# A list of tokens with rows of 64 bytes instead of 4, filled during the scan

## The chip, the core and the metric

The kernel runs on one core of a Trainium2 chip. The core has five engines with queues of their own: TensorE (PE in the profile), VectorE (DVE), ScalarE (ACT), GpSimd (POOL) and SyncE (SP). SP computes nothing here; it issues the plain DMA transfers and loads registers. POOL issues the indirect ones, gathers and scatters whose rows are chosen by indices, beside arithmetic of its own. All transfers run on the same 16 DMA engines. The metric is the device time of one execution, in microseconds. The kernel before took 819.09 us, the median of three runs (815.78 to 823.08).

## The reference

A scan over time with a matrix as state, for 4 x 8 heads, 768 steps and 40 dimensions, and behind it a layer of 8 experts of which each token uses one. In short:

```python
for t in range(S):                                 # S=768, state is D x D for each (batch, head)
    y[:, :, t] = einsum('bhd,bhde->bhe', r[t], state)
    Sa = einsum('bhde,bhe->bhd', state, a[t])
    state = state * w[t][:, :, None, :] - outer(Sa, b[t]) + outer(v[t], k[t])
x = y.transpose(0, 2, 1, 3).reshape(3072, 320)
logits = x @ w_gate + modality_bias[modality_id]   # 8 experts
e_idx = argmax(logits, axis=1)
gate_w = softmax(logits)[arange(N), e_idx]
for e in range(8):
    mask = e_idx == e
    out[mask] = gate_w[mask, None] * (maximum(x[mask] @ w1[e], 0) @ w2[e])   # 320 -> 1024 -> 320
```

## The kernel before

**The scan.** The 768 steps are cut into 24 chunks of 32; two chunks make a pair, for which the inputs are loaded together. Within a chunk the recurrence is solved as a triangular system: a Gram matrix of the inputs is formed on PE (`gram`), masked, written to a scratch tensor in DRAM (`scr`), and read back in another layout (`L<-scr`) for a group of one or two pairs. There it is inverted by elimination (`eliml`, 31 steps of a product and a subtraction: `tmpP`, `L`). The first two groups are eliminated on DVE, the others on POOL (the last one half on each). The result goes out to DRAM (`scrT<-L`), comes back in the layout PE needs (`TT<-scrT`, 32 KB each), and is multiplied into the chunk (`ps_tr<-rs,TT`). There is one buffer for `L`, so the read of the next group waits for the write of this one. Each chunk passes a state `Z` on to the next.

**The gate.** When a pair of chunks is done its outputs `xo` (256 tokens, as two halves of 128 partitions) go through `gate(m,x)`, for m from 0 to 11: logits on PE, the maximum, a one-hot of the expert, and, by products with a triangular matrix and with a running count, the rank of each token within its expert. Expert times 3,072 plus rank is the token's place in the list `lst` in DRAM, `pi`. Two indirect scatters on POOL, one for each half, write the 128 token numbers (`ids`, a constant) to those places. The outputs themselves go to the DRAM tensor `xs`, with the gate's weight in front.

**The list.** `lst` has 29,440 entries of one int32: 8 stretches of 3,072 and a reserve. At the start of the kernel all of it is filled with a number out of range (`BIG`), by one transfer from a tile of 128 x 230; a gather skips such rows. So an expert's tokens can be taken in slots of 256 entries, and places that nobody wrote do no harm. A scatter to `lst` waits until the scatter ahead of it has landed, since both write the same tensor.

**The experts.** A slot takes 256 entries of the list (`idx<-lst`, an SP transfer with a start known only at run time), gathers those rows of `xs` (POOL), splits inputs and weights into two parts for products in fp32r (ACT copies the high part, DVE or POOL subtracts it, L1129 among these), multiplies, and scatters the rows to the output (POOL, L1157). Slots -2 and -1 are prepared within the scan (`early`, after gate m=8, from the 2,304 tokens known by then); their weights lie in tiles that the scan no longer needs. Twelve slots follow. In slot -2 two of the subtractions are given to POOL (`oc=(1,3)`).

**What sets the order.** The scan and the gates are not written in the order they run. A planner (`Sched`) records each instruction with its inputs and outputs, gives each a cost and an urgency (the longest chain of work that hangs on it), and goes forward in modelled time: each engine takes, among the instructions that could start first, the most urgent. SP's transfers share a modelled DMA bandwidth, and a transfer may be put no more than 2 us ahead of it. The order that comes out is fixed for each engine in the program. A transfer that needs nothing and is due late, such as the zeroing of the rows of `xs` that the early slots could touch (`blank`, `xs<-wrm`), is therefore issued when SP has nothing more urgent. Instructions emitted by the planner all have line L381 in the profile. The work of `__init__` comes before the planner's, and the experts' (lines from L1089) are written out by hand.

Of the kernel before, what the change touches and what calls it, by code (L numbers as in the profile page):

```python
# [438 lines left out]
H,S=8,768; XW=324  # L439
# [15 lines left out]
def phase_a(S,ctx,rt,rm,bk,v,w,a,emit_x,pp,ident,kp):  # L455
    nc=S; tc=S.tc; NX=OPT['NX']
# [132 lines left out]
    def xtr(m,q,kd):  # L589
        def one(p):  # L590
            if p==0:
                st['trX']=pst(f"trX{m}_{q}_{kd}",[128,4,4,32])
                if kd==0: st['XT',m,q]=spt("XT",[128,4,4,2,32],f"XT{m}_{q}",OPT['nXT'])
            tr=st['trX']
            nc.tensor.transpose(tr[:,p],st['b',m][:,kd,512*q+128*p:512*q+128*p+128],ident)
            if p==3: nc.scalar.copy(st['XT',m,q][:,:,:,kd,:],tr)
        return [lambda p=p: one(p) for p in range(4)]
# [197 lines left out]
    def go(l):  # L795
        for f in l: f()
# [8 lines left out]
    with contextlib.nullcontext():  # L805
        loadw(0); loada(0); loadb(0); loadw(1)
        go(prep_wl(0,0)); amul(0,0); prep_bk(0,(0,),'b')
        w01=prep_wl(0,1); go(w01[:2]); prep_bk(0,(0,),'k'); go(w01[2:]); amul(0,1); prep_bk(0,(1,))
        loada(1); loadb(1); loadw(2)
        def dums(k_):  # L810
            pass
        go(prep_ab(0,0)); go(xtr(0,0,0)); dums('b'); go(xtr(0,0,1)); dums('c'); g00=gram(0,0); g01=gram(0,1)
        go(prep_ab(0,1)); go(xtr(0,1,0)); go(g00[:7]); go(xtr(0,1,1)); dums('d'); go(prep_wl(1,0)); go(g00[7:]); go(g01[:7]); w11=prep_wl(1,1); go(w11[:3]); go(g01[7:]); go(w11[3:])
        amul(1,0); prep_bk(1,(0,),'b','V'); prep_bk(1,(0,),'k'); amul(1,1); prep_bk(1,(1,))
        e0=eliml(0); e0[0](); loada(2); loadb(2); stack(0); stack(1)
        go(prep_wl(2,0)); go(prep_wl(2,1)); loadw(3); loadr(0); vload(0); vload(1)
        k0=31 if 0 in OPT['HB'] else 6
        go(e0[1:k0])
        go(prep_ab(1,0)); go(xtr(1,0,0)); go(xtr(1,0,1)); dums('e'); go(gram(1,0))
        go(prep_ab(1,1)); go(xtr(1,1,0)); go(xtr(1,1,1)); dums('f'); go(gram(1,1)); dums('g')  # L820
        amul(2,0); prep_bk(2,(0,)); amul(2,1); prep_bk(2,(1,))
        go(prep_ab(2,0)); go(xtr(2,0,0)); go(xtr(2,0,1)); dums('h'); go(gram(2,0)); dums('i')
        go(prep_ab(2,1)); go(xtr(2,1,0)); go(xtr(2,1,1)); go(gram(2,1))
        late2(); loada(3); e1=eliml(1); e1[0](); loadb(3)
        go(e1[1:OPT['EJ']+1])
        go(e0[k0:31]); e0[31](); go(ftr(0)); go(ftr(1)); go(ftr(2)); ttload(0); ttload(1); go(lv(0))
        for q in range(2): go(prep_wl(3,q))
        loadw(4); amul(3,0); amul(3,1); prep_bk(3); loada(4)
        go(prep_ab(3,0)); xg(3,0); go(ftr(3))
        go(e1[OPT['EJ']+1:])  # L830
# [58 lines left out]
PSUM=bass.MemoryType.PSUM; DRAM=bass.MemoryType.DRAM  # L889
NT,D,E,F=3072,320,8,1024  # L890
NTL=NT//128; SL=256; NSL=NT//SL+E-1; NS0=14
LIST=E*NT+NSL*SL; BIG=1<<20
XW=324
MOPT=dict(eb=100,wb=0,em=8,ns0=NS0,gxb=1,MS=('PE','Activation','DVE','Pool'),oc=(0,1,2,3),ow=(),lag=2,pf=0,hb=3,ob=4,
 tb=5,pf0=4, own=[[('q',1),('c',0)],[('c',1)],[('q',2)],[('c',2)],[('q',3)],[('c',3)],[],[]],
# [4 lines left out]
class Moe:  # L900
    def __init__(self,tc,ctx,modality_id,w_gate,mbias,w1,w2,out,ptr,ident):
# [3 lines left out]
        self.gp=ctx.enter_context(tc.tile_pool(name="mgt",bufs=1))  # L905
        dp=ctx.enter_context(tc.tile_pool(name="mdp",bufs=1,space=DRAM))
        self.xs=dp.tile([NT,XW],F32,name="xs")
        self.lst=dp.tile([LIST,1],I32,name="lst")
        self.slt=None

        self.cum=[cp.tile([128,2,E],BF16,name=f"cum{i}") for i in range(2)]
        tctx=ExitStack(); tp=tctx.enter_context(tc.tile_pool(name="mtmp",bufs=1))
        fill=tp.tile([128,LIST//128],I32,tag="fill",name="fill"); nc.gpsimd.memset(fill,BIG)
        nc.sync.dma_start(self.lst.rearrange("(p f) o -> p (f o)",p=128),fill)
        self.wg=cp.tile([128,3,32],F32,name="wg"); nc.gpsimd.memset(self.wg,0.0)
        nc.sync.dma_start(self.wg[:,0:2,0:E],w_gate[0:256].rearrange("(c p) e -> p c e",p=128))
        nc.sync.dma_start(self.wg[64:128,2,0:E],w_gate[256:320])
# [32 lines left out]
        tctx.close()  # L950
        nc.vector.memset(self.cum[0][:,0],0.0); self.S=None
        self.nw=0; self.em=MOPT['em']
    def blank(self,z):

        k=NTL//2-1-self.em
        v=self.xs.rearrange("(c q n) e -> c q (n e)",c=2,q=2)[:,:,64*(self.em+1)*XW:]
        for c in range(2):
            for q in range(2): self.S.sync.dma_start(v[c,q].rearrange("(p a b) -> p a b",p=128,b=81),z[:,0:81].unsqueeze(1).broadcast_to([128,2*k,81]))

    def gate(self,m,x):  # L960
# [34 lines left out]
        pi=t("pi",[128,2],I32)  # L995
        ps=t("ps",[128,2]); nc.vector.tensor_reduce(ps,pv,axis=AX.X,op=ALU.add)
        nc.vector.tensor_copy(pi,ps)
        if m==NTL//2-1: S.boost=1e6
        if m<NTL//2-1: S.slk=SOPT['sll']
        for i in range(2):  # L1000
            nc.gpsimd.indirect_dma_start(self.lst,Off(pi[:,i:i+1].bitcast(U32)),self.ids[:,12*i+m:12*i+m+1],None)
        S.boost=0.0; S.slk=SOPT['slg']
        sm=t("sm",[128,2]); nc.vector.tensor_reduce(sm,ex,axis=AX.X,op=ALU.add)
        nc.vector.tensor_scalar(sm,sm,1e-9,None,op0=ALU.add)
# [48 lines left out]
    def early1(self,R,i,n):  # L1053
# [14 lines left out]
            S.call('sync','load',f,[f"reg{i}_{k}"],[ti])  # L1068
        load(0,LIST-SL); load(1,E-1)
        idx=t("ix",[128,2],I32,2)  # L1070
        S.call('sync','dma_dyn',lambda c,rs: c.sync.dma_start(rs(idx),self.lst[bass.ds(val[i,0],SL)].rearrange("(b p) o -> p (b o)",p=128)),[idx],[f"reg{i}_0",self.lst])
        xg=[S.inst(R[1],f"xg_e{i}{b}",[128,XW],o) for b,o in enumerate([[0,324],[648,972]][i])]
        for b in range(2): nc.gpsimd.indirect_dma_start(xg[b],None,self.xs,Off(idx[:,b:b+1].bitcast(U32)),bounds_check=NT-1,oob_is_err=False)
        self.first.append((idx,xg))
# [2 lines left out]
    def _run(self,ctx,wpool,pool,ph,po):  # L1077
# [12 lines left out]
        def prep(s):  # L1090
            base=nc.values_load(self.tab[0:1,s:s+1],engines=(SP,),min_val=0,max_val=LIST-SL,skip_runtime_bounds_check_because="computed from counts that sum to the number of tokens")
            ex=nc.values_load(self.tab[0:1,NSL+s:NSL+s+1],engines=(SP,),min_val=0,max_val=E-1,skip_runtime_bounds_check_because="clamped to the last expert")
            idx=idxs[s%4]
            nc.sync.dma_start(idx,self.lst[bass.ds(base,SL)].rearrange("(b p) o -> p (b o)",p=128))
            x=xg[s%4]
            if s<4:
                for b in range(2): nc.gpsimd.memset(x[b],0.0)
# [213 lines left out]
```

## Time and profile before

| | |
|---|---|
| median of 3 runs | 819.09 us |
| profiled execution, time | 814.86 us |
| its span, first to last instruction | 812.9 us |
| mean granted TensorE clock | 0.826 |
| busy: PE, DVE, ACT, POOL | 598.3, 504.5, 388.1, 273.5 us |
| list scatters | 24, first 184.92 us, last 578.63 us |
| `idx<-lst` | 12 in the experts, 2 early |
| DMA engines, mean share by queue | SP's 53.1%, POOL's 3.0% |

Times within the profile are microseconds from the start of the span. A row of the timeline has start, length, engine, line, operation, the tile written and the tiles read, the count, and in brackets the idle time of the engine before it and what ended that. A row of the waits has the engine, the line and what it wanted, what it waited for, then the total, the number of times and the longest. In the list of DMA issues the last number of POOL's rows is the median time from the issue to the landing. "issue" as a releaser means that the profile shows nothing that the engine waited for.

### The profile page before, as it was taken

How to read it: one execution, taken by the hardware profiler on the slowest of the kernel's cores; microseconds unless marked ns; L12 is line 12 of the kernel's file. 1: busy time of each engine (PE TensorE's matmuls, PEld its weight loads, DVE VectorE, ACT ScalarE, POOL GpSimd, SP SyncE). 2: the span in 40 equal slices, each digit the busy share in tenths (PEclk: the TensorE clock that was granted, in tenths of full speed). 3: DMA queues.
4: the chain of work that ended last, by engine and by line, in shares of the span. 5: the costliest groups of instructions: out<-in, count | busy, mean ns of one | idle time of the engine just before them, and what ended most of it. 6: DMA issues, size and time to landing. Idle time of an engine off the chain costs nothing. (4 is left out here: it accounts for less than half of the span.)

```text
span 812.9 us, 25308 instructions
## 1 busy us (share of the span) xinstructions
PE 598.3 (74%) x10527; PEld 535.1 (66%) x10527; DVE 504.5 (62%) x1260; ACT 388.1 (48%) x814; POOL 273.5 (34%) x435
## 2 busy tenths in 40 slices
PE   0652789946577677778824677885679999999992
PEld 0542677835566566666614556764679999999992
DVE  5694845863248846675621563656768888888850
ACT  1662154731457355554521524543546666666640
POOL 8440038314181582055625300200234222322210
PEclk9966586876879899797955757986889999999997
DMA  2979231555726529663479557736099755776500
GB/s 57 334 221 165 64 74 47 176 156 46 46 68 179 166 62 149 132 104 54 62 55 60 51 35 123 196 45 143 18 303 283 224 174 184 238 234 213 178 33 14
DMA packets 103480, 104.97 MB, mean 129 GB/s; under 512 B 65806, under 2 KB 86464, under 8 KB 101824
## 3 DMA queue, kind: packets, MB, share of 16 engines
q1 hardware_dynamic: 99904, 95.35, 53.1%
q0 software_dynamic: 3456, 7.93, 3.0%
q8 instruction: 85, 1.39, 1.1%
q14 instruction: 35, 0.29, 0.1%
HBM read 88.46 MB, written 15.99 MB: 128 GB/s over the span
## 5 line engine op out<-in xcount | busy, mean ns | idle before, releaser
L381 POOL TENSOR_TENSOR tmpP<-L 128x30 f32<-128x30 f32 (+9 forms) x135 | 70.8, 525 | 165.2 <-DMA L<-scr 155.5
L381 ACT COPY XZ<-BK 32x640 f32<-32x640 f32 x96 | 69.4, 723 | 31.9 <-PE ps_tr L381 22.1
L381 POOL TENSOR_TENSOR L<-L,tmpP 128x30 f32<-128x30 f32 (+9 forms) x135 | 73.4, 544 | 9.9
L381 POOL DMA_INDIRECT lst<-ids,pi x24 | 24.5, 1023 | 153.9 <-DMA lst<-ids,pi 69.5
L1150 PE MATMUL os<-l,hh 128*128 128x320 f32 x208 | 65.7, 316 | 11.5 <-POOL l L1129 11.3
L381 PE MATMUL ps_tr<-rs,TT 64*64 64x40 f32 x896 | 42.0, 256 | 42.6 <-DMA TT<-scrT 35.1
L1142 ACT ACTIVATE hh<-h 128x256 fp32r<-128x256 f32 x104 | 40.0, 384 | 68.9 <-PE h L1138 68.7
L381 DVE COPY U<-ps_tr 32x320 f32<-32x320 f32 x56 | 27.6, 492 | 70.2 <-PE ps_tr L381 53.8
L381 PEld LDWEIGHTS ps_tr<-rs,TT 64*64 64x64 f32 x896 | 37.8, 166 | 49.3 <-DMA TT<-scrT 25.2
L1138 PE MATMUL h<-xh,h 128*128 128x256 f32 x224 | 66.9, 299 | 2.2 <-ACT h L1120 1.4
L1151 PE MATMUL os<-h,hl 128*128 128x320 f32 x208 | 65.1, 313 | 0.0
L1138 PE MATMUL h<-xh,l 128*128 128x256 f32 x224 | 64.9, 290 | 0.3 <-DVE l L1121 0.3
L1149 PE MATMUL os<-h,hh 128*128 128x320 f32 x208 | 64.9, 312 | 0.0
L1138 PE MATMUL h<-xl,h 128*128 128x256 f32 x224 | 64.5, 288 | 0.0
L381 ACT COPY U<-ps_tr 32x320 f32<-32x320 f32 x56 | 23.3, 415 | 83.9 <-DVE U L381 54.3
L381 DVE TENSOR_TENSOR xo<-ps_tr,H 32x320 f32<-32x320 f32 x96 | 46.7, 487 | 24.9 <-PE ps_tr L381 14.6
L1143 DVE SCALAR_TENSOR_TENSOR hl<-h,hh 128x256 fp32r<-128x256 f32 x104 | 44.0, 423 | 24.4 <-ACT hh L1142 23.2
L1157 POOL DMA_INDIRECT out_dram<-o,idx x24 | 26.9, 1123 | 90.8 <-DVE hl L1143 29.2
L381 PE MATMUL ps_tr<-ident,BK 128*128 128x128 f32 x192 | 38.8, 354 | 15.7 <-DVE BK L381 11.9
L381 ACT COPY XZ<-ps_tr 40x320 f32<-40x320 f32 x92 | 38.6, 420 | 20.8 <-PE ps_tr L381 19.4
L381 PE MATMUL tz<-U,XZ 64*40 64x40 f32 x1472 | 32.4, 234 | 21.5 <-ACT U L381 8.5
L1150 PEld LDWEIGHTS os<-l,hh 128*128 128x128 f32 x208 | 40.0, 192 | 12.2 <-POOL l L1129 11.8
(204 smaller groups left out, 1687.4 us busy)
## 6 DMA issues: line engine op xcount, KB each, us to landing
r<-in_moe_w_dram SPq DMA_DIRECT2D x13, 1280.0 KB
r<-in_moe_w_dram SPq DMA_DIRECT2D x13, 1024.0 KB
BK<-in_bk_dram SPq DMA_DIRECT2D x12, 1024.0 KB
r<-in_moe_w_dram SPq DMA_DIRECT2D x26, 256.0 KB
A<-in_a_dram SPq DMA_DIRECT2D x12, 512.0 KB
U<-in_v_dram SPq DMA_DIRECT2D x48, 128.0 KB
ws<-in_w_dram SPq DMA_DIRECT2D x24, 165.5 KB
xs<-xo SPq DMA_DIRECT2D x24, 162.0 KB
```

Of the source, the lines that this page charges most:

```text
L381: else: r=getattr(getattr(nc,eng),name)(*[rs(x) for x in a],**{n:rs(x) for n,x in k.items()})
L1138: for i,(a,b) in enumerate(k): nc.tensor.matmul(hp,a,b,start=(i==0),stop=(i==len(k)-1))
L1142: nc.scalar.activation(hh,hp,AF.Relu)
L1143: nc.vector.scalar_tensor_tensor(hl,hp,0.0,hh.bitcast(F32),op0=ALU.max,op1=ALU.subtract)
L1149: nc.tensor.matmul(os[b],hh[:,sl],h2[:,f],start=(f==0),stop=False)
L1150: nc.tensor.matmul(os[b],hh[:,sl],l2[:,f],start=False,stop=False)
L1151: nc.tensor.matmul(os[b],hl[:,sl],h2[:,f],start=False,stop=(f==7))
L1157: nc.gpsimd.indirect_dma_start(self.out,bass.IndirectOffsetOnAxis(ap=idx[:,b:b+1].bitcast(U32),axis=0),o,None,bounds_check=NT-1,oob_is_err ...
```

## The change

A row of `lst` gets 16 int32 columns, 64 bytes, of which only the first is read. The gate copies the token numbers of its two halves to a tile of 128 x 2 x 16 on DVE (`idw`), each number 16 times, and a scatter writes rows of 16. The reads of the list take column 0, so they still move 256 elements of 4 bytes, now 64 bytes apart.

The list is 16 times as large, 1.88 MB. It is no longer filled in `__init__` but by a method `fill`, recorded with the planner among the loads of the third pair of chunks: one SP transfer that writes a tile of 128 x 115 (460 bytes a partition, set once) 32 times over to each partition's share. The tile is kept instead of being given back after `__init__`. What is computed is the same.

```diff
-        go(prep_ab(2,1)); go(xtr(2,1,0)); go(xtr(2,1,1)); go(gram(2,1))
+        emit_x.fill(); go(prep_ab(2,1)); go(xtr(2,1,0)); go(xtr(2,1,1)); go(gram(2,1))
...
-LIST=E*NT+NSL*SL; BIG=1<<20
+LW=16; LIST=E*NT+NSL*SL; BIG=1<<20
...
-        self.lst=dp.tile([LIST,1],I32,name="lst")
+        self.lst=dp.tile([LIST,LW],I32,name="lst")
...
-        fill=tp.tile([128,LIST//128],I32,tag="fill",name="fill"); nc.gpsimd.memset(fill,BIG)
-        nc.sync.dma_start(self.lst.rearrange("(p f) o -> p (f o)",p=128),fill)
+        self.fw=LIST//256; self.fil=cp.tile([128,self.fw],I32,name="fill"); nc.gpsimd.memset(self.fil,BIG)
...
+    def fill(self):
+
+        self.S.sync.dma_start(self.lst.rearrange("n o -> (n o)").rearrange("(p r f) -> p r f",p=128,r=2*LW),self.fil.unsqueeze(1).broadcast_to([128,2*LW,self.fw]))
...
+        idw=t("idw",[128,2,LW],I32); nc.vector.tensor_copy(idw,self.ids[:,m:m+13:12].unsqueeze(2).broadcast_to([128,2,LW]))
...
-            nc.gpsimd.indirect_dma_start(self.lst,Off(pi[:,i:i+1].bitcast(U32)),self.ids[:,12*i+m:12*i+m+1],None)
+            nc.gpsimd.indirect_dma_start(self.lst,Off(pi[:,i:i+1].bitcast(U32)),idw[:,i],None)
...
-        S.call('sync','dma_dyn',lambda c,rs: c.sync.dma_start(rs(idx),self.lst[bass.ds(val[i,0],SL)].rearrange("(b p) o -> p (b o)",p=128)),[idx],[f"reg{i}_0",self.lst])
+        S.call('sync','dma_dyn',lambda c,rs: c.sync.dma_start(rs(idx),self.lst[bass.ds(val[i,0],SL),0:1].rearrange("(b p) o -> p (b o)",p=128)),[idx],[f"reg{i}_0",self.lst])
...
-            nc.sync.dma_start(idx,self.lst[bass.ds(base,SL)].rearrange("(b p) o -> p (b o)",p=128))
+            nc.sync.dma_start(idx,self.lst[bass.ds(base,SL),0:1].rearrange("(b p) o -> p (b o)",p=128))
```

## The prediction

> **What bounds the kernel now.** I read the page first, for where the tensor engine (PE) is full and where it is not.
>
> ```profile
> span 812.9 us, 25308 instructions
> PE   0652789946577677778824677885679999999992
> ```
>
> A slice is 20.3 us. From slice 30 (about 595 us) PE is full to the end: the expert stage is bound by PE there, and nothing in the change touches it. The open time lies before, in the scan. So the next view was the waits in total, and then the DMA issues with their time to landing.
>
> ```profile
> POOL lst L381 <- DMA lst<-ids,pi: 69.5, 9, 10.4
> POOL lst L381 <- issue: 40.4, 8, 12.0
> PE os L1150 <- POOL l L1129: 11.3, 2, 6.2
> ...
> lst<-ids,pi POOLq DMA_INDIRECT x24, 10.0
> out_dram<-o,idx POOLq DMA_INDIRECT x24, 3.7
> ```
>
> GpSimd (POOL) stands 109.9 us in front of list scatters, in 17 waits, because a scatter may not start before the one ahead has landed (the profile names no releaser for the second row, but its waits have the same length). A list scatter takes 10.0 us to land though it writes 128 times 4 bytes; the scatter of output rows, also 128 writes but of 1,280 bytes each, takes 3.7. More bytes land sooner, so the 10 us belongs to the 4-byte write and not to the issue on POOL or the count of rows.
>
> Whether that costs time is read from the stages. I laid the timeline of POOL beside windows of all engines:
>
> ```profile
> 184.92 1.17 POOL L381 DMA_INDIRECT lst<-ids,pi  x1 [0.17 <-DVE U L381]
> 197.71 1.01 POOL L381 DMA_INDIRECT lst<-ids,pi  x1 [9.81 <-issue]
> 209.88 1.00 POOL L381 DMA_INDIRECT lst<-ids,pi  x1 [6.80 <-DMA lst<-ids,pi]
> ...
> 398.24 1.00 POOL L381 DMA_INDIRECT lst<-ids,pi  x1 [0.23 <-DVE pv L381]
> 408.80 1.00 POOL L381 DMA_INDIRECT lst<-ids,pi  x1 [8.11 <-DMA lst<-ids,pi]
> 421.04 1.00 POOL L381 DMA_INDIRECT lst<-ids,pi  x1 [8.54 <-DMA lst<-ids,pi]
> ...
> 476.95 1.00 POOL L381 DMA_INDIRECT lst<-ids,pi  x1 [11.79 <-DVE e_n L381]
> ```
>
> The windows' columns are length, then busy us of PE, its weight loads, DVE, ACT and POOL, the clock, the DMA share and GB/s:
>
> ```profile
> 192.00:197.50 5.50, 0.00 (x0) 0.00 (x0) 0.00 (x0) 0.00 (x0) 0.00 (x0) 0.80 0.26 22
> 218.50:222.50 4.00, 0.00 (x0) 0.00 (x0) 0.00 (x0) 0.00 (x0) 0.00 (x0) 1.00 0.83 38
> 404.50:408.50 4.00, 0.00 (x0) 0.00 (x0) 0.00 (x0) 0.00 (x0) 0.00 (x0) 0.80 0.62 33
> 418.50:434.50 16.00, 0.00 (x0) 0.00 (x0) 0.00 (x0) 0.00 (x0) 1.00 (x1) 0.50 0.78 55
> 486.00:489.00 3.00, 0.00 (x0) 0.00 (x0) 0.00 (x0) 0.00 (x0) 0.00 (x0) 0.97 0.65 33
> ...
> 184.92:590.00 405.08, 281.07 (x6628) 236.83 (x6629) 219.97 (x600) 180.53 (x381) 139.73 (x235) 0.78 0.57 90
> 100.00:184.92 84.92, 67.89 (x1655) 57.27 (x1655) 52.90 (x128) 43.41 (x92) 36.31 (x73) 0.76 0.40 112
> ```
>
> Five times every engine stops. Each stop lies inside the 11 us after a scatter (from 184.92, 209.88, 398.24, 408.80 with 421.04, and 476.95), and next to no bytes move meanwhile (22 to 55 GB/s). So a scatter in flight holds up not only POOL but the other transfers, and with them whatever waits for those. The last two rows give the same as a rate: PE is busy 0.80 of the scan before the first scatter, and 0.69 from there to 590.
>
> **Part 1: the scatter lands sooner.** Nothing in this trace writes 64-byte rows to memory. Below, the nearest are writes in runs of 128 bytes (a block of 32 floats), two issues of 512 runs each:
>
> ```profile
> 107.56 0.86 SPq L381 DMA_DIRECT2D scr<-G  x2
> ...
> 109.94 0.34 SPq L381 DMA_DIRECT2D L<-scr  x1
> ```
>
> The read L<-scr needs what these write, so 1,024 runs of 128 bytes landed within 2.4 us of the first issue. From above it is the 10.0 us of today. I take 3.8, next to the 3.7 of the output scatter, which is of the same kind and count; so each of 24 landings loses 6.2 us, with 2.4 and 10.0 as the ends. POOL's own instruction stays near 1.0 us.
>
> The Trainium skill speaks against this. Its page "DMA: Bandwidth & Descriptors", section Specifications, has 512 bytes as the least transfer for full rate, with a read-modify-write below it. By that rule 64 bytes is no better than 4, and the landing stays at 10.0. The 128-byte rows above bear it out badly. It is a rival below.
>
> Each stop can lose what its scatters lose, at most its own length: 5.5 + 4.0 + 4.0 + 3.0 for the four that are shorter than 6.2, and 2 x 6.2 = 12.4 of the 16.0, which has two scatters in it. Its chain is this:
>
> ```profile
> 412.53 0.35 SPq L381 DMA_DIRECT2D scrT<-L  x1
> ...
> 421.96 0.32 SPq L381 DMA_DIRECT2D TT<-scrT  x1
> ...
> 434.98 1.28 PE L381 MATMUL ps_tr<-rs,TT 64*64 64x40 f32 x14 [17.07 <-DMA TT<-scrT]
> ```
>
> The eliminated block is written out, read back and used, each a transfer, and a scatter runs beside the first and another beside the second. Further down the same two legs are quoted without a scatter (97.81 to 100.89 for the write): 3.1 us instead of 9.4, with half the bytes. The five stops give 28.9 us. What could come late next is the block itself: it is computed on POOL, and it too is held by the scatters, so it moves earlier with them. I take the 28.9 whole and leave out the smaller gaps (PE alone idle), to pay for what surfaces behind. Ends: 10 us, if the recurrence of the scan takes up two thirds; and the whole loss of rate, 405.08 - 281.07 / 0.80 = 53.5 us, which has part 2's first stall in it.
>
> **Part 2: the passage to the experts.** The last gate's two scatters stand in POOL's queue in front of two subtractions (L1129) of the first expert's weights:
>
> ```profile
> 568.70 1.33 POOL L381 DMA_INDIRECT lst<-ids,pi  x1 [11.79 <-DVE w L1125]
> 578.63 1.06 POOL L381 DMA_INDIRECT lst<-ids,pi  x1 [8.60 <-DMA lst<-ids,pi]
> ...
> 591.25 1.26 POOL L1099 DMA_INDIRECT xg<-xs,idx  x1 [9.23 <-issue]
> ...
> 588.25 0.38 SPq L1094 DMA_DIRECT2D idx<-lst  x1
> ...
> 581.46 0.64 PE L1150 MATMUL os<-l,hh 128*128 128x320 f32 x1 [6.22 <-POOL l L1129]
> ...
> 595.45 0.63 PE L1150 MATMUL os<-l,hh 128*128 128x320 f32 x1 [5.07 <-POOL l L1129]
> ```
>
> With 3.8 the second scatter goes at 572.5, the first subtraction ends at 575.6 instead of 581.4, and PE's 6.2 us goes. The list's read follows its last landing: 576 instead of 588.25, the gather 579 instead of 591.25, and the second subtraction is done 12 us earlier against a PE that comes 6.2 earlier, so the 5.1 goes too. Together 11.3 us. Next late would be DVE's copies of the same weights; PE is full from 595 on.
>
> **Part 3: the fill.** It writes 1.88 MB in 4,096 runs of 460 bytes instead of 118 KB once at the start. It needs nothing from the scan and is due at the first scatter (184.92). The planner treats the zeroing of the token rows (xs<-wrm) alike, which is due later still, and issues it when SP first has nothing more pressing, so I expect the fill just there, ahead of it:
>
> ```profile
> xs<-wrm SPq DMA_DIRECT2D x4, 243.0 KB
> ...
> 65.03 1.29 SPq L381 DMA_DIRECT2D xs<-wrm  x2
> ...
> 67.30 1.14 SPq L381 DMA_DIRECT2D scrT<-L  x1
> ...
> 76.64 5.88 SPq L381 DMA_DIRECT2D TT<-scrT  x8
> ...
> 97.81 0.51 SPq L381 DMA_DIRECT2D scrT<-L  x1
> ...
> 100.89 4.15 SPq L381 DMA_DIRECT2D TT<-scrT  x8
> ```
>
> This is a bad place: scrT to TT takes 9.3 us beside the zeroing and 3.1 without, and all of PE waits. 972 KB in 3,072 runs cost 6.3 us; the fill costs 6.3 x 4096/3072 = 8.3 by runs, 6.3 x 1.94 = 12.1 by bytes. If it pushes the zeroing behind the reads, 6.3 comes back. Ends 0 (a slot where nothing hurries) and 12.1; I take the middle, 6. Queued behind it on SP's rings: A, scrT, and the TT reads.
>
> **Part 4: the copies and the reads.** Twelve copies of 128x32 on DVE:
>
> ```profile
> 417.83 0.17 DVE L381 COPY xo<-sm 128x8 f32<-128x8 f32 x1
> ```
>
> At 0.2 us each that is 2.4 us, of a DVE busy 220 of 405 us; the copies read only constants and can go in any gap. The scatter waits for them, but they stand long before it. I take 1, ends 0 and 2.4. The list's reads stay 256 elements of 4 bytes, now 64 apart: 3.0 us today (588.25 to 591.25), taken as unchanged, a microsecond either way.
>
> **Sum.** -28.9 - 11.3 + 6 + 1 = -33.2. The profiled execution took 814.86 us (span 812.9), so 781.7; the median of the three runs, 819.09, is 4.2 above that execution, so 786 in its terms, and all times below are in its terms.
>
> **Rivals.**
> - *The scan gives more.* All of the lost rate comes back: 53.5 + 5.1 - 7 = 51.6, so 767. For it: POOL's 109.9 us of waits, much of it inside the elimination that PE then waits for. Against: the recurrence, which also holds the scan before the first scatter at 0.80.
> - *Only the passage gains.* The stops come back behind something else in the same order of work: -11.3 + 7, so 815, no measurable change. For it: the order on every engine is planned anew with a 1.88 MB transfer and twelve copies in it. Against: in the stops nothing is running that could be the next bound.
> - *The 64-byte write is no faster, and the fill is paid.* Place: the TT reads at 76.64, behind the fill; price 12.1 + 1, so 832. It decides from the point where the gain of 40.2 x (10 - L)/6.2 for a landing of L falls under 13.1, a landing above 8.0 us. For it: the fill lies in a stretch where all wait for DMA. Against: the 128-byte runs. It is also what would happen if the wider rows did not reach the memory as whole 64-byte writes. This is where the 512-byte rule of the Trainium skill leads ("DMA: Bandwidth & Descriptors", Specifications).
>
> **How the numbers follow.** Forecast 0.62; more from the scan 0.13; passage only 0.12; no faster write 0.10; 0.03 for a new order that gains elsewhere. About 1% (8 us) is what a measurement of this kernel can tell from no change. Faster: 0.62 + 0.13 + 0.03 = 0.78; within 1%: 0.12 less a little that ends above, 0.11; slower 0.11. The range goes from 760 (53.5 + 5.1 with a fill that costs nothing) to 815 (passage only); outside lie the slow write and a little of each end.
>
> **What would show it.** Right: landing of the list scatter near 4 us; POOL's waits for it under 40 us in total; the five stops gone or short; PE's wait for L1129 near 0; fill issued near 65 us, and the TT wait behind it longer than today. Wrong: landing near 10 us (part 1 falls, with all that hangs on it); landing short, but PE's share of the scan still 0.69 (the stops were not the scatters'); a fill before 60 us or one that holds up more than 12.

## The result, and the profile after

The kernel after takes 739.61 us (median of four runs, 735.12 to 742.28), the kernel before 817.43 in the same series (808.56 to 823.08). The ratio is 0.908, interval 0.897 to 0.918: 78 us faster, where the prediction had 33. The profiled execution of the kernel after took 742.25 us, its span is 740.5.

From the page of the kernel after, the span and PE in 40 slices, here of 18.5 us:

```profile
span 740.5 us, 25338 instructions
...
PE   0564178984788779757978688857999999999991
```

PE is full from slice 28, about 518 us on; before, its last long wait ended at 595.45. What follows is unchanged work: PE's last 1,500 products take 195.3 us in both kernels. So the time was won ahead of that. Four stretches show where: up to the first product with `TT`, from there to the first list scatter, from there to the last product with `TT` (the scan beside the scatters), and the rest. The windows of before, then of after, with the columns of the prediction (length, busy us of PE, weight loads, DVE, ACT, POOL, then clock, DMA share, GB/s):

```profile
0.00:82.55 82.55, 32.10 (x406) 26.55 (x406) 55.59 (x159) 35.81 (x60) 35.98 (x68) 0.81 0.72 192
82.55:184.92 102.37, 82.57 (x1966) 69.83 (x1970) 67.54 (x201) 46.72 (x100) 36.31 (x73) 0.72 0.37 103
184.92:542.33 357.41, 249.44 (x6259) 209.62 (x6260) 187.30 (x500) 157.18 (x324) 132.59 (x226) 0.78 0.60 92
542.33:812.90 270.57, 234.21 (x1902) 229.08 (x1901) 194.10 (x404) 148.38 (x330) 68.64 (x68) 0.93 0.56 169
```

```profile
0.00:89.25 89.25, 32.62 (x414) 27.38 (x414) 60.63 (x169) 35.82 (x60) 36.42 (x68) 0.80 0.76 188
89.25:187.90 98.65, 75.91 (x1950) 64.50 (x1951) 63.99 (x192) 45.63 (x98) 35.26 (x69) 0.76 0.50 114
187.90:478.30 290.40, 230.97 (x6291) 196.34 (x6287) 186.34 (x503) 158.69 (x329) 133.46 (x231) 0.84 0.43 114
478.30:740.50 262.20, 231.73 (x1881) 226.49 (x1880) 195.69 (x410) 146.98 (x327) 69.89 (x68) 0.94 0.56 175
```

The differences are +6.7, -3.7, -67.0 and -8.4, together the -72.4 by which the spans differ. The third is the one to explain. PE's share there rises from 0.70 to 0.80, which is its share before the first scatter. PE stands idle 108.0 us in it before and 59.4 after, 48.5 less; and it is busy 18.5 us less with nearly the same number of products (6,259 and 6,291), because the granted clock rose from 0.78 to 0.84 (249.4 x 0.78 / 0.84 = 231.6).

The scatters themselves, in the DMA issues of after:

```profile
lst<-fill SPq DMA_DIRECT2D x1, 1840.0 KB
...
lst<-idw,pi POOLq DMA_INDIRECT x24, 2.8
```

and four of them on POOL, where one follows another within a gate:

```profile
187.88 1.17 POOL L381 DMA_INDIRECT lst<-idw,pi  x1 [0.17 <-issue]
191.34 1.00 POOL L381 DMA_INDIRECT lst<-idw,pi  x1 [0.92 <-DMA lst<-idw,pi]
197.29 1.00 POOL L381 DMA_INDIRECT lst<-idw,pi  x1 [0.17 <-issue]
200.76 1.00 POOL L381 DMA_INDIRECT lst<-idw,pi  x1 [0.57 <-DMA lst<-idw,pi]
```

They land after 2.8 us instead of 10.0 (medians of the landings that the traces show, 14 of 24 after and 3 of 24 before), and POOL's wait for the one ahead is under 1 us here, where it was 6 to 10. In the waits of after, in total:

```profile
PE ps_tr L381 <- DMA Fg<-H: 17.1, 2, 16.8
PE ps_tr L381 <- issue: 16.9, 21, 2.6
...
POOL lst L381 <- DMA lst<-idw,pi: 12.8, 8, 4.5
...
PE ps_tr L381 <- DMA TT<-scrT: 8.5, 4, 3.2
...
PE ps_rp L381 <- issue: 7.2, 9, 2.7
...
PE tz L381 <- issue: 1.5, 4, 0.5
...
POOL lst L381 <- issue: 0.8, 5, 0.2
```

and the rows of before that answer to PE's:

```profile
PE ps_tr L381 <- DMA TT<-scrT: 35.1, 3, 17.1
...
PE ps_tr L381 <- issue: 32.1, 16, 5.9
...
PE ps_rp L381 <- issue: 23.1, 10, 9.4
...
PE tz L381 <- issue: 6.2, 5, 2.0
```

POOL's 109.9 us before list scatters are 13.6. PE's wait for the block that comes back (`TT`) falls from 35.1 us to 8.5, but not all of that is gained: 12.2 of the 35.1 are the wait for the first block of all, ahead of the scatters, and in after PE's wait at that place is put down to `Fg<-H` (16.8 us, in the first row above). In the third stretch alone the wait for `TT` falls from 17.1 to 3.8. PE's idle time that the profile puts down to no releaser ("issue") goes from 61.4 us (32.1 + 23.1 + 6.2) to 25.6 (16.9 + 7.2 + 1.5). In the third stretch it is 56.3 before and 18.1 after. 25.0 of the 56.3 lie in four of the five stops that the prediction had priced, as the first experiment shows; the other 31.3 are smaller gaps, for which it had no term. There is no row of PE waiting for the subtractions of the first expert on POOL any more.

The fill went where the prediction put it. SP and PE in the timeline of after:

```profile
64.94 0.64 SPq L381 DMA_DIRECT2D lst<-fill  x1
65.69 7.56 SPq L381 DMA_DIRECT2D scrT<-L  x1
...
85.50 4.30 SPq L381 DMA_DIRECT2D TT<-scrT  x8
89.25 2.38 PE L381 MATMUL ps_tr<-rs,TT 64*64 64x40 f32 x32 [1.49 <-DMA TT<-scrT]
...
90.88 1.28 SPq L381 DMA_DIRECT2D xs<-wrm  x2
```

The write of the block (scrT) takes 7.56 us behind it, the read starts 19.8 us after the write instead of 9.3, and the first product comes at 89.25 instead of 82.55, though the zeroing of `xs` was pushed behind it.

### The profile page after: what moved, and what is told of

Same layout as the page of the kernel before. It is cut to its first block, busy times and chain, and to the rows that moved or that the text cites. A ratio compares the mean times of both kernels' runs of the same rounds, so it can differ in the third digit from the quotient of the medians.

```text
span 740.5 us, 25338 instructions
## 1 busy us (share of the span) xinstructions
PE 571.2 (77%) x10527; PEld 514.7 (70%) x10527; DVE 506.6 (68%) x1272; ACT 387.1 (52%) x814; POOL 275.0 (37%) x435
## 5 line engine op out<-in xcount | busy, mean ns | idle before, releaser
L1145 ACT ACTIVATE hh<-h 128x256 fp32r<-128x256 f32 x104 | 40.0, 384 | 62.7 <-PE h L1141 62.2
L1160 POOL DMA_INDIRECT out_dram<-o,idx x24 | 25.1, 1044 | 97.2 <-DVE o L1159 29.9
L381 POOL DMA_INDIRECT lst<-idw,pi x24 | 24.6, 1024 | 87.6 <-DVE pi L381 55.1
L381 PE MATMUL ps_tr<-rs,TT 64*64 64x40 f32 x896 | 40.5, 249 | 15.5 <-DMA TT<-scrT 8.5
L1102 POOL DMA_INDIRECT xg<-xs,idx x24 | 29.9, 1244 | 49.5 <-DMA idx<-lst 26.6
L381 PE MATMUL ps_tr<-ident,BK 128*128 128x128 f32 x192 | 33.9, 317 | 17.5 <-DVE BK L381 11.9
L381 DVE TENSOR_TENSOR MB<-ps_tr,msk 64x512 f32<-64x512 f32 x48 | 33.0, 687 | 19.3 <-PE ps_tr L381 17.3
```

The lines of the kernel that those rows point to most:

```text
L381: else: r=getattr(getattr(nc,eng),name)(*[rs(x) for x in a],**{n:rs(x) for n,x in k.items()})
L1102: nc.gpsimd.indirect_dma_start(x[b],None,self.xs,bass.IndirectOffsetOnAxis(ap=idx[:,b:b+1].bitcast(U32),axis=0),bounds_check=NT-1,oob_is_e ...
L1145: nc.scalar.activation(hh,hp,AF.Relu)
L1160: nc.gpsimd.indirect_dma_start(self.out,bass.IndirectOffsetOnAxis(ap=idx[:,b:b+1].bitcast(U32),axis=0),o,None,bounds_check=NT-1,oob_is_err ...
```

## The experiments

The change does several things at once: it shortens the landing, it fills 16 times as much, it puts a copy before each gate's scatters, and it makes the planner plan every engine anew, so that most instructions stand elsewhere than before. The experiments take these apart. In most of them the planner's order is that of one of the two kernels, kept exactly, and only what a planned instruction reads or writes is exchanged when it is written out. Where a kernel was timed four times its runs lie 6 to 15 us apart; a time of one run is read to no better than that. "Before" is always its median on the same chip.

### The wide rows in the order of before

The list has rows of 64 bytes, the gate's copy stands in front of the gate's maximum, and the fill is among the first transfers. All else is in the order of before.

```diff
-        nc.sync.dma_start(self.lst.rearrange("(p f) o -> p (f o)",p=128),fill)
+        # behind the other loads of __init__, into rows of LW=16
+        nc.sync.dma_start(self.lstw.rearrange("n o -> (n o)").rearrange("(p r f) -> p r f",p=128,r=2*LW),fill.unsqueeze(1).broadcast_to([128,2*LW,self.fw]))
...
-            nc.gpsimd.indirect_dma_start(self.lst,Off(pi[:,i:i+1].bitcast(U32)),self.ids[:,12*i+m:12*i+m+1],None)
+            # idw: both halves' numbers, 16 times each, copied on DVE in front of the gate's maximum
+            nc.gpsimd.indirect_dma_start(self.lstw,Off(pi[:,i:i+1].bitcast(U32)),self.idw[n%2][:,i],None)
```

> The kernel before with its order of work in the scan kept on every engine; only the list is wide (64-byte rows, copied by DVE early in each gate, filled at the start of the kernel, where the trace of before shows the DMA idle from 10 to 17 us). Theory A, the landing of the scatters alone makes the gain: landing near 2.8 us and 735 to 750 us. Rival B, a good part of the gain is the new order that the planner made once the fill and twelve copies were among its instructions: the five stops and the passage alone go, 817 - 29 - 11, so 770 to 785.

Measured: 720.90 us (four runs, 717.67 to 727.88) against 814.04, ratio 0.889 [0.882, 0.895], 14 us below the range that was expected. A repetition beside other kernels:

> e1_old_order_wide once more, beside the other widths on the same chip: 715 to 728 us. In the call before, e8_fill_behind_loads took 731.9 with the same order of work; if this lies there too, chips and layouts make 10 us, and the place of the fill within the first loads is worth nothing that shows.

Measured: 723.23 (720.71 to 728.48) against 811.29, ratio 0.893 [0.886, 0.899]. So the faster landing, with the order of before, is worth some 90 us. This kernel is faster than the change itself by 16 to 19 us in the bare times, by 12 to 15 when each is set against its own before (ratios 0.889 and 0.893 against 0.908; the interval of the second touches that of the change). The new order is not where the gain comes from.

Since the order is kept, PE's products can be followed one by one from the profile of before to this one. These are PE's waits in before at four of the prediction's five stops; the fifth, 17.07 us at 434.98, stands in the prediction:

```profile
197.62 0.22 PE L381 MATMUL ps_rp<-U,G 32*32 32x40 f32 x1 [5.71 <-issue]
...
227.46 1.29 PE L381 MATMUL ps_rp<-Z,ATb 128*64 128x40 f32 x18 [9.37 <-issue]
...
408.65 0.49 PE L381 MATMUL ps_tr<-XZ,MB 104*32 104x40 f32 x16 [4.30 <-issue]
...
491.49 0.34 PE L381 MATMUL ps_tr<-RT,UT 128*64 128x64 f32 x1 [5.59 <-issue]
```

PE stands still longer than the window in which every engine does: 42.0 us at these five products, where the prediction took 28.9. With the short waits of the products just around them it is 45.8 us before and 4.2 here. All other waits of PE in the third stretch add up to 62.2 us before and 47.5 here. The third stretch of this kernel, with the columns as above:

```profile
184.86:458.68 273.82, 222.08 (x6260) 187.49 (x6260) 189.23 (x510) 155.98 (x324) 134.06 (x226) 0.89 0.45 120
```

It is 83.6 us shorter than before. Of this 41.6 us come from the five stops, 14.7 from the smaller gaps, and 27.4 from PE's own work (249.44 to 222.08 us for the same products), as the granted clock goes from 0.78 to 0.89.

### The 4-byte rows in the order of after

The reverse: the order of after, with its copies and its fill (which goes to a tensor that nobody reads), but the scatters write one column to a list of 4-byte rows, filled at the start as before.

```diff
-            nc.gpsimd.indirect_dma_start(self.lst,Off(pi[:,i:i+1].bitcast(U32)),idw[:,i],None)
+            nc.gpsimd.indirect_dma_start(self.lstn,Off(pi[:,i:i+1].bitcast(U32)),idw[:,i,0:1],None)
```

> The changed kernel with its order of work in the scan kept; at emission the scatters write 4-byte rows of a second, narrow list, filled at the start as before, and the 1.88 MB fill goes to a tensor that nobody reads. Theory A: landing near 10 us and the time of before plus the fill's 7 us, 815 to 830. Rival B: the order keeps its part of the gain, 775 to 795.

Measured: 850.18 us (846.10 to 856.15) against 814.04, ratio 1.043 [1.038, 1.049], 20 us above the range that was expected. With the slow landing the new order, with its copies and its fill, is 36 us worse than the old one; 7 of them are there by the first product with `TT` (89.64 against 82.55), behind the fill. The waits of this kernel:

```profile
DVE idw L382 <- DMA lstn<-idw,pi: 77.0, 6, 17.7
...
POOL lstn L382 <- DMA lstn<-idw,pi: 58.0, 7, 9.9
...
POOL lstn L382 <- issue: 44.2, 8, 10.2
```

The new row is the first. The planner put each gate's copy early, so DVE stands at it until a buffer of `idw` comes free, which is when an earlier gate's scatters have landed. With a landing of 2.8 us that wait is 2.6 us in all, in the kernel after. What the copies cost thus depends on the landing. How much of the 36 us is this wait no run isolates.

### No scatters

As the first experiment, without the 24 list scatters and without the copies for them. Then no token is found, and the experts' rows are not written to the output, so transfers in the expert stage are missing too.

> As e1_old_order_wide, but no gate scatters to the list, so that no token is found in it and no output row is written: the time of the scan without any scatter, in the old order. Theory A: the floor that a fast landing can reach, within 10 us of e1_old_order_wide. If wide scatters still hold up other work, it lies 15 us or more below that run. Look at the scan alone (first use of TT to the last), since the experts have less to transfer.

Measured: 717.01 us (one run) against 814.04. It is a floor for what the scatters can cost in this order, though its expert stage has lighter traffic: the wide scatters, at 720.9, lie 4 us over it, which is within what one run can tell.

### POOL's wait or the write in flight

Two things could make the slow landing dear: POOL waits for it, and the write in flight holds up other transfers. In this kernel, in the order of before and with 4-byte rows, each gate's second scatter goes to a tensor of its own, so that two scatters to the same tensor are a whole gate apart. Half of the tokens are then missing from the list.

```diff
+            f=self.lst[:] if i else self.lst
+            if i: S.swap[id(f)]=self.lstb
-            nc.gpsimd.indirect_dma_start(self.lst,Off(pi[:,i:i+1].bitcast(U32)),self.ids[:,12*i+m:12*i+m+1],None)
+            nc.gpsimd.indirect_dma_start(f,Off(pi[:,i:i+1].bitcast(U32)),self.ids[:,12*i+m:12*i+m+1],None)
```

> The kernel before, its order kept, with 4-byte rows; the second scatter of each gate goes to a tensor of its own that nobody reads, so it need not wait for the first. Half of the tokens are missing from the list and get no output. All 24 narrow writes stay. If the loss is POOL's waiting, POOL's waits for a landing go and the scan gets 40 us or more shorter (760 to 780 in all). If the narrow writes hold up the other transfers wherever they fly, the scan stays within 20 us of before (795 to 820).

Measured: 773.92 us (one run) against 814.04. The waits:

```profile
PE ps_tr L385 <- issue: 31.3, 16, 5.2
...
PE ps_tr L385 <- DMA TT<-scrT: 20.4, 5, 11.9
...
PE ps_rp L385 <- issue: 15.9, 12, 5.6
...
PE tz L385 <- issue: 4.8, 3, 1.7
...
POOL lstb L385 <- issue: 2.3, 11, 0.3
...
POOL lst L385 <- issue: 1.3, 5, 0.5
...
POOL lstb L385 <- DMA lstb<-ids,pi: 0.9, 1, 0.9
```

POOL's 109.9 us of waiting are 4.5, and PE's wait for `TT` falls from 35.1 to 20.4. The time is 40 us less. The third stretch of this kernel:

```profile
180.20:512.18 331.98, 252.68 (x6259) 214.91 (x6256) 187.48 (x499) 157.74 (x324) 132.08 (x226) 0.78 0.56 98
```

It is 25.4 us shorter than before. PE's idle time falls by 28.7 us, at the five stops from 45.8 to 16.2, and its other waits are still 63.1 us (62.2 before). The clock is 0.78 as before, and PE's work takes 252.7 us (249.4 before). In the first experiment, with the wide rows, these three are 4.2, 47.5 and 222.1. So of the 93 us between before and that kernel (814.0 to 720.9), some 40 go with POOL's waits; the other 53 are still there when nobody waits for the writes any more, and are gone when the writes are wide. Two reservations belong to this split: the two scatters of a gate are now in flight together (the two landings of `lstb` that the trace shows took 11.2 and 17.4 us), and half of the tokens are missing in the expert stage.

### Writes that nobody waits for

The first experiment's kernel, with a third scatter in each gate to a tensor that nobody reads: 128 writes of 4 bytes to the same places, or of 64 bytes.

```diff
+            # behind the gate's two scatters
+            nc.gpsimd.indirect_dma_start(self.lstb,Off(pi[:,0:1].bitcast(U32)),self.ids[:,m:m+1],None)
```

> As e1_old_order_wide (720.9 us), with a third scatter behind the two of each gate: 128 times 4 bytes, with the same indices, into a tensor that nobody reads and for whose landing nothing waits but the next of its kind, a gate later. So POOL pays about 1 us a gate, and what is more is what a narrow write in flight does to others. If it holds up the other transfers: 12 x 3 to 4 us more, so 755 to 770, with stops of all engines behind the decoys. If the cost of before was POOL's waiting alone: 721 to 735.

> The same with decoys of 64-byte rows: what the third scatter costs by itself. Both theories: 721 to 735. The difference to e7_decoy_narrow is the price of 12 narrow writes that nobody waits for.

Measured, one run each on one chip (before 816.54): 776.08 with the narrow ones, 741.76 with the wide ones, each 6 to 7 us above what was expected. Twelve narrow writes cost 34.3 us more than twelve wide ones, 2.9 us each, and nothing in the program waits for either. For 24 that would be 69 us, against the 53 that the last experiment left over. POOL's waits for list scatters to land hardly differ (17.0 us with the narrow ones, 13.2 with the wide ones). The third stretch differs by 31.3 us: PE is idle 75.2 us in it against 58.2, and busy 252.4 against 238.1 with the same products, at a clock of 0.80 against 0.85. One such place in the timeline of the narrow ones:

```profile
301.44 1.13 POOL L1010 DMA_INDIRECT lstb<-ids,pi  x1 [0.31 <-issue]
...
308.03 1.08 SPq L386 DMA_DIRECT2D U<-in_v_dram  x2
...
314.80 0.74 PE L386 MATMUL ps_tr<-XZ,MB 128*32 128x40 f32 x27 [5.07 <-issue]
...
315.58 0.48 DVE L386 TENSOR_TENSOR xo<-ps_tr,H 32x320 f32<-32x320 f32 x1 [6.51 <-DMA U<-in_v_dram]
```

A load of SP's is issued at 308.03, DVE gets it after 6.5 us of idleness, and PE stops in the middle of a row of equal products for 5.07 us with nothing that the profile names. The scatter ahead is one that nobody reads. With the wide decoys the same product follows after 0.20 us.

The wide decoys are not free either: 741.8 is 19 to 21 us over the kernel without them (720.9 and 723.2 on other chips), 1.5 to 1.7 us a scatter, more than the 1 us of POOL's instruction and more than expected.

### Small writes, or neighbours

So far wide and narrow differ in two things: the size of a write, and how many entries lie close together. The rank of a token is the number of tokens that its expert had before, so the 128 entries of a scatter form at most 8 runs of neighbours, on average 16 long or more. Here the list has the wide rows but a scatter writes only the first 4 bytes of each: the list is seen as one column and the index is multiplied by 16. There are no copies.

```diff
-        nc.vector.tensor_copy(pi,ps)
+        nc.vector.tensor_scalar(pi,ps,16.0,None,op0=ALU.mult)
...
-            nc.gpsimd.indirect_dma_start(self.lst,Off(pi[:,i:i+1].bitcast(U32)),self.ids[:,12*i+m:12*i+m+1],None)
+            nc.gpsimd.indirect_dma_start(self.lstw.rearrange("n o -> (n o)").unsqueeze(1),Off(pi[:,i:i+1].bitcast(U32)),self.ids[:,12*i+m:12*i+m+1],None)
```

> As e1_old_order_wide, but a scatter writes only the first 4 bytes of each 64-byte row. If a write of less than a whole 64 bytes is slow by itself: landing near 10 us and 800 to 830 us. If it is slow because neighbours in the list share 64 bytes (the ranks of one expert's tokens follow each other): landing near 2.8 us and 715 to 735 us.

Measured: 723.28 us (one run) against 811.29; the writes of the repetition with wide rows gave 723.23 on the same chip. In the DMA issues:

```profile
lstw<-ids,pi POOLq DMA_INDIRECT x24, 2.8
```

A write of 4 bytes is as good as one of 64. Not the size of the write is what costs, but the neighbours.

The same kernel with the entries 4, 8, 16 and 32 bytes apart, the first as the control:

> Four-byte writes without copies, in the form of the run with narrow writes in wide rows, but with rows of 4 bytes: the order of before, one fill of 115 KB among the kernel's first loads, the list seen as one column. Control: if only the spacing of the entries matters, this is the kernel before in all that counts: landing 10 us, 805 to 820 us. If the other parts of that form (the fill's place, the form of the index) had a share in its gain, it comes out below 800.

> The same with entries 8 bytes apart, so that 8 entries share 64 bytes and each write touches 4 of 8 bytes. If neighbours within 64 bytes are written one after another: landing 10.0 - (10.0 - 2.8) x 8/15 = about 6, time about 723 + (6 - 2.8)/7.2 x 91 = 765. If only words that touch each other collide: landing near 2.8, 723. If a unit is smaller than 64 bytes, 32 say, still 4 share it: landing between 3 and 7.

> Entries 16 bytes apart, 4 share 64 bytes. Neighbours within 64 bytes one after another: landing about 10.0 - 7.2 x 12/15 = 4.2, time about 741. Units of 32 bytes: 2 share one, landing 3.3, about 730. Only touching words: 2.8, 723.

> Entries 32 bytes apart, 2 share 64 bytes. Neighbours within 64 bytes one after another: landing about 10.0 - 7.2 x 14/15 = 3.3, time about 729 less what the smaller fill gives (0 to 5). Units of 32 bytes or less: 2.8, 718 to 723. The run with rows of 32 bytes written whole took 719, so no more than that is expected of the spacing alone.

The rows of the four, in this order, with the landing at the end:

```profile
lstw<-ids,pi POOLq DMA_INDIRECT x24, 11.0
```

```profile
lstw<-ids,pi POOLq DMA_INDIRECT x24, 6.7
```

```profile
lstw<-ids,pi POOLq DMA_INDIRECT x24, 4.2
```

```profile
lstw<-ids,pi POOLq DMA_INDIRECT x24, 3.0
```

| bytes between entries | landing | time, one run | PE's idle time without a releaser |
|---|---|---|---|
| 4 | 11.0 us | 810.27 us | 60.0 us |
| 8 | 6.7 | 756.66 | 38.9 |
| 16 | 4.2 | 725.58 | 18.9 |
| 32 | 3.0 | 723.17 | 18.6 |
| 64 (another chip) | 2.8 | 723.28 | 13.0 |

(The last column is the sum of the three rows of PE with "issue" shown above, in each kernel. Before on the chip of the first four: 805.39, one run. The landings are medians of the 5, 10, 21, 18 and 21 that the traces show.) The control is the kernel before in all but its form, and takes its time. The landing falls with the number of neighbours in the way of entries that share a small piece of memory and are written one after another: with pieces of 32 bytes, 8, 4, 2, 1 and 1 entries share one, and 1.85 + 1.14 for each gives 11.0, 6.4, 4.1, 3.0 and 3.0; with pieces of 64 bytes, 16 to 1 entries, 2.25 + 0.55 for each gives 11.1, 6.7, 4.5, 3.4 and 2.8. These are fits; which of the two it is the runs do not tell, and none shows such a piece by itself. The time falls by 12.5 us for each microsecond of landing from 11.0 to 6.7, and by 12.4 from 6.7 to 4.2, and then not at all within what one run can tell.

The spacing has made the list larger, too. To part the two, the decoys once more, with 4-byte writes into one small tensor: 128 numbers at two runs of 64 consecutive places, or with the index times 16, in two regions of 4 KB.

```diff
-            nc.gpsimd.indirect_dma_start(self.lstb,Off(pi[:,0:1].bitcast(U32)),self.ids[:,m:m+1],None)
+            # idd: ids times 1, or times 16, set once
+            nc.gpsimd.indirect_dma_start(self.lstb,Off(self.idd[:,m:m+1].bitcast(U32)),self.ids[:,m:m+1],None)
```

> The version with the order of before and 64-byte rows, plus one decoy of 128 four-byte writes a gate that nobody reads or waits for, as in the run with narrow decoys, but to two runs of 64 consecutive places (16 entries share each 64 bytes). If sharing is the cause: as the narrow decoys at the ranks' places, 776, within 10, since there too an expert's entries are adjacent.

> The same decoy with its index times 16: 128 four-byte writes, each in 64 bytes of its own, in one region of 8 KB. If sharing 64 bytes is the cause: as the wide decoys, 742, within 8. If it is that the writes fall close together in memory, or that four bytes are written, it stays near 776.

Measured, one run each on one chip (before 828.66, one run, the highest of all): 790.03 adjacent, 742.03 spread. Forty-eight microseconds lie between two kernels that differ in one factor of an index, 4.0 us for each scatter; the spread ones are at the time of the 64-byte decoys (741.76). The adjacent ones are 4 us above the end of what was expected; without a landing for them in the trace it stays open whether that is the chip or the longer runs of neighbours. That the writes fall in a small region is not the cause, and that they are of 4 bytes is not either.

### The width of a row

If 64 bytes are enough, are 32? And what do 128 do?

```diff
-LW=16
+LW=8     # and LW=32
```

> As e1_old_order_wide with rows of 32 bytes, so half the fill. If 32 bytes are written as a whole: landing near 2.8 us, the fill's 3 to 4 us at the start gone, 714 to 722 us. If two rows in one 64 bytes disturb each other as sixteen did: landing between 3 and 10 us, 725 to 790.

> As e1_old_order_wide with rows of 128 bytes: landing 2.8 us as with 64, and a fill of 3.8 MB that takes some 15 us longer at the start: 730 to 742 us.

Measured beside the repetition (723.23): rows of 32 bytes 718.96 (four runs, 715.01 to 726.29), ratio 0.883 [0.876, 0.890] without the highest of them, landing 2.9; rows of 128 bytes 732.79 (one run), landing 3.0. The landing no longer changes, and the fill grows: 0.94, 1.88 and 3.77 MB. The 32-byte rows are the fastest kernel that computes everything, but their interval overlaps with that of the 64-byte rows.

### The place of the fill

In the order of before, with the fill behind the first loads of the scan instead of ahead of them; and in the order of after, with the fill in that same place instead of at 65 us.

```diff
     def loadb(m):
-        t=st['b',m]=Br[m%len(Br)]; nc.sync.dma_start(t,bk[m])
+        t=st['b',m]=Br[m%len(Br)]
+        # for m=0 the fill is issued here, ahead of this load
+        nc.sync.dma_start(t,bk[m])
```

> As e1_old_order_wide, but the fill stands on SP behind the first loads of the decay and of A and ahead of the first load of b and k, where the trace of before shows the DMA idle for 7 us. In e1_old_order_wide it stands ahead of those loads, and PE's first use of TT came at 86.2 us instead of 82.6. Expected: first use at 82 to 84, and 715 to 721 us. If the fill is not hidden there, no change or slower by up to 4 us.

> The changed kernel with its order of work, wide list; the planner sees the fill where it was, but at emission it stands at the place of e8_fill_behind_loads instead of at 65 us. The changed kernel took 739.6 us and e1_old_order_wide 720.9. If the fill's place makes that difference (6.7 us in the wait for the first TT and what follows from it): 721 to 733. If the new order itself is slower: 733 to 739.

Measured on one chip (before 816.54): 731.91 (729.70 to 735.43), ratio 0.899 [0.892, 0.905], in the order of before, and 728.58 (723.92 to 733.09), ratio 0.892 [0.885, 0.900], in the order of after. The first was meant to be better than the fill ahead of everything and is not: 732 against 721 and 723 on other chips. Its profiled run has its first product with `TT` earlier (84.41 against 86.19) and loses that later, in a scan of the same order, for a reason that I did not find. The second is 11 us faster than the kernel after (739.61, before 817.43), from which it differs in the place of the fill alone; the two intervals of the ratio just overlap, but its first product with `TT` comes at 81.37 instead of 89.25. And with the fill in the same place the two orders are 3 us apart, with intervals that overlap: with a fast landing the new order is worth nothing that shows.

## Why the prediction was wrong in size, step by step

**Landing.** Predicted 3.8 us from the output scatter, measured 2.8. The 4-byte scatter was the trouble, as the comparison of 128 x 4 with 128 x 1,280 bytes said. But the reason was taken to lie in the write's size, and it lies in the neighbours: 4-byte writes 64 bytes apart land in 2.8 us. In the rows that served as bounds one entry fills 128 or 1,280 bytes, so no two of them start within 64 bytes either, and they bounded the landing well. That the forecast came near is in part luck: the change made the entries wider and set them apart in one step.

**Part 1, the scan: this is the term that failed.** It had 28.9 us, from five stops in which every engine is idle, and left the smaller gaps out, "PE alone idle", to pay for what would surface behind. Nothing of that size surfaced. The stretch lost 67.0 us (-70.7 with the one ahead of the first scatter): 48.5 of PE's idle time and 18.5 of its busy time. With the order of before, where each term can be followed, three things were mis-sized. The five stops gave 41.6 us and not 28.9: each was capped at the window in which all engines are idle, or at 6.2 us for a landing, while PE stood still for 42.0 there. (The prediction puts them inside the 11 us after a scatter; they end 10.3 to 13.5 us after it.) The smaller gaps, counted as nothing, gave 14.7. And PE's own work, taken as fixed, gave 27.4 at the higher clock. The prediction's other measure, the rate, had the idle time nearly: 53.5 us if PE's share went from 0.69 back to 0.80. The share did that, and PE's idle time in the stretch fell by 48.5. What the rate could not show is the clock. By landing, the forecast counted 40.2 us for 6.2, 6.5 us for each microsecond; the spacings from 4 to 16 bytes show about 12.

That the smaller gaps and the clock belong to the scatters is shown by two of the experiments. Narrow writes that nobody waits for cost 2.9 us each over wide ones, about half of it PE's idle time and half a lower clock; and with POOL's waits taken away, PE's smaller gaps (63.1 us) and the clock (0.78) stay as they were until the writes have no neighbours. The prediction had said that a scatter in flight holds up the other transfers, but charged this only where everything stood still. Many of the gaps have no releaser in the profile. That they are waits for instructions or for data that come by the held DMA queues is a guess; the profile shows that the gaps shrink with the landing, not what ends them. Why the clock falls while such writes are in flight stays open, too. It does not follow PE's idle time as a sum: with 4-byte entries 8 bytes apart PE is idle 77 us in the third stretch and busy 234, with the two tensors idle 79 and busy 253. What goes with it in all twenty profiles is the number of long waits: where PE has four or more single waits over 3 us in that stretch (7 before, 5 with the two tensors, 4 with the narrow decoys), its work there takes 249 to 263 us; where it has at most one (the kernel after, the first experiment, the wide decoys), 222 to 240. No run changes these waits alone, so that they are the cause is not shown. And the clock differs somewhat without any scatter: in the second stretch it is 0.72 before, 0.76 after, 0.74 in the first experiment and 0.78 with the two tensors.

**Part 2, the passage.** Predicted -11.3, measured -8.4 in the last stretch (-13.6 in the order of before), with PE's wait for POOL's subtraction gone as said. The list's read stayed cheap: its issue at 512.38, the gather of the rows at 515.06, 2.7 us against 3.0 before. In the timeline of after:

```profile
512.38 0.37 SPq L1097 DMA_DIRECT2D idx<-lst  x1
...
515.06 1.49 POOL L1102 DMA_INDIRECT xg<-xs,idx  x1 [6.22 <-issue]
```

**Part 3, the fill.** Predicted at `xs<-wrm`'s place near 65 us for 6 us; found at 64.94, and the start came out 6.7 us later. The net size is right by luck: the zeroing did move behind the reads, which should have given 6.3 back, so by the prediction's own sum the fill cost 13.0 in gross, more than either of the two estimates, by runs and by bytes. (The one by bytes mixes two units; with 1,840 and 972 KB it is 11.9 and not 12.1.) In the other place, at the start, the kernel is 11 us faster, 7.9 of them by the first product.

**Part 4, the copies.** Predicted 1 us; DVE is busy 2.1 us more in all, and one wait of 2.6 us for a buffer is new. At this landing it is in the noise; at a landing of 11 us the same copies cost DVE 77 us of waiting.

**The rivals.** "The scan gives more" was the right one in kind, and its 767 was still 27 us above the median: the clock, with 18.5 us in the third stretch, is most of what is missing. "Only the passage gains" fell, since nothing took the place of the stops. The rival with the 64-byte write no faster fell with the landing. The Trainium skill ("DMA: Bandwidth & Descriptors", section Specifications) puts the limit at 512 bytes, with a read-modify-write below. Here 4, 32, 64 and 128 bytes a row all land in 2.8 to 3.0 us once they stand 32 bytes or more apart, so the size by itself is not what these scatters pay for. A read-modify-write that neighbours in one piece must do in turn would fit the spacings; that is argued and not shown.

Of the sum, -28.9 became -70.7, -11.3 became -8.4, and the +7 of fill and copies +6.7 for both: -72.4 instead of -33.2.

## What to carry to other kernels

When a scatter of small entries to memory is slow, look at how close its entries lie: here a spacing of 16 bytes, by a factor on the index (and a list with rows that wide), gave nearly all of the gain, without wider writes. Price a slow transfer by the whole loss of rate in the stages where it is in flight (PE's share beside a stage without it), not by the stops that can be pinned to it, and a stop by the time for which PE stands still; a write of neighbours that nobody waits for cost 3 to 4 us here. Such a sum leaves out the clock, which a stage without the transfer does not price either: ahead of the first scatter it was 0.72, below the 0.78 beside the scatters. And look separately at where a one-time fill lands: some 11 us of this change were given back by its place.

## What the runs showed of the hardware

An indirect scatter of 128 entries of 4 bytes lands in 11.0, 6.7, 4.2, 3.0 and 2.8 us at 4, 8, 16, 32 and 64 bytes between neighbouring entries, and in 2.8 us at 64 bytes whether 4 or 64 bytes are written at each. While such a scatter of neighbours is in flight, other work is held up: 2.9 us for each scatter at the ranks' places over the same scatter with rows of 64 bytes, 4.0 at consecutive places over the same scatter with entries 64 bytes apart (one run of each). The granted clock of the span goes with the spacing: 0.815 at a spacing of 4 bytes, 0.864 at 8, 0.870 to 0.880 from 16 on, and PE's busy time for the same products goes from 604.7 to 568.9 us.
